# Attention with grouped heads: a strip of every sixth score chunk exponentiated on VectorE, and PV three chunks behind

## The chip, the core and the metric

The kernel runs on one core of one Trainium2 chip. The metric is the device time in microseconds (us); a shorter time is better. A core has five engines that run side by side and meet through semaphores: TensorE (PE in the profile; its weight loads are listed apart as PEld), VectorE (DVE), ScalarE (ACT), GpSimd (POOL) and the sync engine (SP), which here only issues transfers. Matmul results land in PSUM, which has eight banks of 512 fp32 columns on 128 partitions; everything else is in SBUF.

## What is computed

```python
B, Hq, Hkv, Sq, Sk, D = 16, 32, 8, 288, 512, 128      # q, k, v in bf16
k = jnp.repeat(k, Hq // Hkv, axis=1)
v = jnp.repeat(v, Hq // Hkv, axis=1)
scores = jnp.einsum("bhqd,bhkd->bhqk", q, k) * D ** -0.5
p = jax.nn.softmax(scores, axis=-1)
return jnp.einsum("bhqk,bhkd->bhqd", p, v)
```

Four query heads share one k and v head. The inputs are small (normal values times 0.05), so the exponentials are taken without subtracting a maximum; the kernel checks the sums at its end and has a slow general path (lines 17 to 121) for inputs where that fails.

## The kernel before

**Tiling.** A group is one k/v head of one batch: 128 groups (`NG`). Its four query heads give 1152 query rows, held as 9 tiles of 128. A chunk is three of these tiles (`TPC`), 384 query rows, against all 512 keys, which are four key tiles of 128 (`NJ`). Scores are computed transposed, with keys on the partitions, so a chunk has 4 x 384 = 1536 score columns (`CH`), three PSUM banks. There are three chunks in a group and `NS` = 384 in all, numbered n.

**Stages of a chunk.**
- S(n), `op_s`, matmuls on line 361: six matmuls into `ps_s[:, n % 2]`, cut at bank and key-tile borders (384, 128, 256, 256, 128 and 384 columns). They need k and q in SBUF, transposed by DMA, and exp(n-2) finished, since `ps_s` has two buffers.
- exp(n), `op_exp`, line 417 (line 411 for the first bank of chunk 0): one ScalarE instruction over all 1536 columns, from PSUM to bf16 in `pt_sb[:, n % NPT]`, with `NPT` = 4 buffers, so it also needs PV(n-4) finished.
- PV(r), `op_pv`, line 384: twelve matmuls (four key tiles by three query tiles) with 128x128 of `pt_sb` as weights and 129 columns of v as the moving operand. The 129th column of v is all ones, so it sums the exponentials. The result, 3 x 129 = 387 columns, goes to `ps_o[:, r % 2]`, one bank each. PV(r) waits for exp(r), for v, and for the eviction of r-2, which frees the bank. The last chunk's PV is written apart (`op_pv_last`, line 395, in `ps_s`).
- VectorE, lines 434 and 444: `op_rc` takes the reciprocals of the three sums, `op_ev` multiplies the outputs by them and writes bf16 to `o_sb`, the eviction. Once every 24 chunks two small reductions (`op_stat`) keep the largest and smallest reciprocal.

**Order.** Each engine's instructions are written out in one fixed order. TensorE (line 515 on) issues S(n) and then PV(n-LAG), with `LAG` = 2. ScalarE issues exp(n) for all n. VectorE loops over r with `op_rc(r)` and `op_ev(r)`. A wait is put into an instruction only if the engine hasn't seen that count before (`need`). SP's transfers are sorted by a time in chunks that the code works out for each (lines 488 to 500): k and v for four groups at a time (`UG`) into three slots, q for one group into twelve slots (`NQ`), and the store of one group, whose time has `LAG` in it. GpSimd copies v into its slot with the ones column (`op_vc`, line 427), one group at a time, as soon as the load of four groups has landed and the slot's last PV is done.

**Start.** Before the loop TensorE runs warm-up matmuls on zeros (`op_warm`) and transposes the k of group 0 itself (`op_kt`, line 336), which VectorE copies to `kt_sb` (`op_kc`, line 343). The k of group 1 is transposed in the loop at n = LAG. Their loads, and that of v for groups 0 and 1, are issued from ScalarE's queue (lines 533 to 536), ahead of its first exponential.

Of the kernel before, what the change touches and what calls it, by code (L numbers as in the profile page):

```python
# [1 line left out]

# [7 lines left out]
FP32 = mybir.dt.float32  # L10
I32 = mybir.dt.int32
# [109 lines left out]
    return {"pool": on_pool, "sp": on_sync, "pe": on_tensor, "dve": on_vector, "act": on_scalar}  # L121


def bass_standalone__gqa_softmax__near_ridge_kernel(
    nc: bass.Bass,
    q: bass.AP,
# [6 lines left out]
    P = 128  # L133
    R = (Hq // Hkv) * Sq
    NJ = Sk // P
# [9 lines left out]
    assert COLS % CH == 0 and NT == NC * TPC and NJ * P == BANK  # L145
    scale = float(D) ** -0.5
    DV = D + 1
    VP = 160
    LAG = 2
    TW = TPC * P  # L150
    UG = 4
    NU = NG // UG
    NSLOT = 3
    NQ = 12
    NPT = 4
    WARM = 5
    AHEAD = 1.08
    NO = 12
    NS = NG * NC
# [10 lines left out]
    with ExitStack() as es:  # L170
# [14 lines left out]
            S("us_v%d" % i)  # L185
        for i in range(UG):
            S("s_k%d" % i)
        for name in ["s_v0", "s_v2", "s_s0", "s_kd0", "s_kd1", "s_id", "s_kp"]:
            S(name)
        for i in range(NQ):  # L190
            S("s_q%d" % i)
# [36 lines left out]
        st_sb = main.enter_context(nc.sbuf_tensor("st_sb", [P, 2, B], FP32))  # L228
        ck_sb = main.enter_context(nc.sbuf_tensor("ck_sb", [P, 3], FP32))
        bad_sb = main.enter_context(nc.sbuf_tensor("bad_sb", [P, 2, ALONE + 1], FP32))  # L230
        one_f = main.enter_context(nc.sbuf_tensor("one_f", [P, 1], FP32))
        z_sb = main.enter_context(nc.sbuf_tensor("z_sb", [P, BANK], BF16))
        dum = main.enter_context(nc.sbuf_tensor("dum", [P, 2], FP32))
# [5 lines left out]
        def need(eng, waits):  # L239

            left = []
            for (s, n) in waits:
                key = (id(eng), s)
                if seen.get(key, 0) < n:
                    seen[key] = n
                    left.append((sem[s], n))
            return left

        def emit(eng, waits, fn):
            waits = need(eng, waits)  # L250
            for (s, n) in waits[:-1]:
                eng.wait_ge(s, n)
            ins = fn()
            if waits:
                ins.wait_op(waits[-1][0], waits[-1][1], "sem-ge")
            return ins
# [17 lines left out]
        def op_v(u, eng=None, g0=0, g1=UG):  # L274
            eng = eng or nc.sync
            sl = u % NSLOT
            if u >= NSLOT:
                for (s, n) in need(eng, [("s_vc", UG * (u - NSLOT + 1))]):
                    eng.wait_ge(s, n)
            eng.dma_start(  # L280
                vd_sb[:, sl, g0:g1], v_v[:, u * UG + g0:u * UG + g1]
            ).then_inc(sem["us_v%d" % sl if u > 0 else "s_v%d" % g0], 16)
# [63 lines left out]
        def op_warm(n, w, dst):  # L346

            for x in range(n):
                emit(nc.tensor, [("s_z", 1)], lambda: nc.tensor.matmul(  # L349
                    dst[:, 0:w], z_sb[:, 0:P], z_sb[:, 0:w], start=True, stop=True))  # L350

        def op_s(n):
            eng = nc.tensor
            g, i = n // NC, n % NC
            sl, gi = (g // UG) % NSLOT, g % UG
            waits = [have("k", g), have_q(g, i)]
            if n >= 2:
                waits.append(("s_e", n - 1))
            qg = qt_sb[:, g % NQ, i * TPC:(i + 1) * TPC].rearrange("d t p -> d (t p)")
            for x, (c, j, r0, w) in enumerate(pieces):  # L360
                ins = emit(eng, waits if x == 0 else [], lambda: eng.matmul(  # L361
                    ps_s[:, n % 2, c:c + w], kt_sb[:, sl, j, gi, :], qg[:, r0:r0 + w], start=True, stop=True))
                if n == 0 and c + w == BANK:
                    ins.then_inc(sem["s_s0"], 1)
            ins.then_inc(sem["s_s"], 1)

        def outs(r):

# [4 lines left out]
        def op_pv(r):  # L373
            eng = nc.tensor
            g = r // NC
            sl, gi = (g // UG) % NSLOT, g % UG
            waits = [("s_vc", g + 1), ("s_e", r + 1)]
            if 2 <= r < NS - 1:
                waits.append(("s_ev", r - 1))


            for j in range(NJ):
                for a in range(TPC):
                    ins = emit(eng, waits if a == 0 and j == 0 else [], lambda: eng.matmul(  # L384
                        outs(r)[:, a, :], pt_sb[:, r % NPT, j, a * P:(a + 1) * P],
                        v_sb[:, sl, gi * NJ + j, 0:DV], start=(j == 0 and a == 0), stop=(j == NJ - 1),
                        skip_group_check=True))
            ins.then_inc(sem["s_pv"], 1)
# [13 lines left out]
        def op_exp(n):  # L402
            eng = nc.scalar
            waits = [("s_s", n + 1)]
            if n >= NPT:
                waits.insert(0, ("s_pv", n - NPT + 1))
            dst, src = pt_sb[:, n % NPT], ps_s[:, n % 2].rearrange("p (j r) -> p j r", r=TW)
            parts = [(dst.rearrange("p j r -> p (j r)"), ps_s[:, n % 2])]
            if n == 0:
                d, s = parts[0]  # L410
                emit(eng, [("s_s0", 1)], lambda: eng.activation(d[:, 0:BANK], s[:, 0:BANK], ACTF.Exp, scale=scale))  # L411
                parts = [(d[:, BANK:CH], s[:, BANK:CH])]
            if n == NS - 1:
                w = TW - P
                parts = [(dst[:, :, 0:w], src[:, :, 0:w]), (dst[:, :, w:TW], src[:, :, w:TW])]
            for (d, s) in parts:
                emit(eng, waits, lambda: eng.activation(d, s, ACTF.Exp, scale=scale)).then_inc(sem["s_e"], 1)  # L417


        def op_vc(g):  # L420
# [11 lines left out]
        def op_rc(r):  # L432
            eng = nc.vector
            emit(eng, [("s_pv", r + 1)], lambda: eng.reciprocal(  # L434
                rl_sb[:, TPC * r:TPC * (r + 1)].unsqueeze(2), outs(r)[:, :, D:DV])).then_inc(sem["s_rc"], 1)
# [74 lines left out]
        @block.tensor  # L510
        def _(eng):
            op_warm(WARM, BANK, ps_o[:, 1])
            op_kt(0, range(NJ), 0)
            op_warm(6, P, ps_s[:, 1])
            for n in range(NS):
                if n == LAG:
                    op_kt(1, range(NJ), 1)
                    op_warm(4, P, ps_o[:, 0])
                op_s(n)
                if n >= LAG:  # L520
                    op_pv(n - LAG)
            for r in range(NS - LAG, NS - 1):
                op_pv(r)
            for a in range(TPC):
                op_pv_last(a)
            emit(eng, [("s_ev", NS - 1), ("s_bad", 2)], lambda: eng.matmul(  # L526
                ps_o[0:1, NS % 2, 0:ALONE + 1], one_f[:], bad_sb[:, 1, :], start=True, stop=True)
            ).then_inc(sem["s_bad"], 1)
            choose(eng, "pe")

        @block.scalar
        def _(eng):
            op_kd(eng, 0)
            emit(eng, [("s_one", 1)], lambda: eng.activation(dum[:, 1:2], dum[:, 0:1], ACTF.Exp))  # L534
            op_v(0, eng, 0, 2)
            op_kd(eng, 1)
            for n in range(NS):
                op_exp(n)
            op_ev_act()
            choose(eng, "act")  # L540
# [12 lines left out]
        @block.vector  # L553
        def _(eng):
            eng.memset(z_sb[:], 0.0).then_inc(sem["s_z"], 1)  # L555
            eng.memset(dum[:], 0.0).then_inc(sem["s_one"], 1)
            eng.memset(one_f[:], 1.0)
            op_kc(0, range(NJ), 0, 1)
            op_kc(1, range(NJ), 1, 2)
            per_b = G * NC  # L560
            w0 = NS - 1 - ALONE // TPC
            last = rl_sb[:, NG * NT - ALONE:NG * NT]
            for r in range(NS - 1):
                op_rc(r)
                op_ev(r)
                if r % per_b == per_b - 1 and r < NS - 1:
                    op_stat(r // per_b)
                if r == w0:
                    op_stat(B - 1)
                if r == w0 + 1:  # L570
                    emit(eng, [("s_stat", B)], lambda: eng.tensor_reduce(
                        ck_sb[:, 0:1], st_sb[:, 0, :], AX.X, ALU.max))
                    eng.tensor_reduce(ck_sb[:, 1:2], st_sb[:, 1, :], AX.X, ALU.min).then_inc(sem["s_stat"], 1)
                if r == w0 + 2:
                    op_over(ck_sb[:, 0:1], ck_sb[:, 1:2], ALONE, ALONE + 1, ("s_stat", B + 1), B + 2)
            op_rc(NS - 1)
            op_ev_last()
            op_over(last, last, 0, ALONE, ("s_rc", NS), B + 3)
            with nc.allow_low_precision(reason="a count of at most 2048"):
                emit(eng, [("s_bad", 3)], lambda: eng.tensor_reduce(  # L580
                    flag_i[:], ps_o[0:1, NS % 2, 0:ALONE + 1], AX.X, ALU.add)).then_inc(sem["s_flag"], 1)
            choose(eng, "dve")
# [30 lines left out]
```

## Time and profile before

| | us |
|---|---|
| median of 4 runs | 528.7 (527.38 to 529.08) |
| the profiled execution: its time | 527.63 |
| the profiled execution: its span, from the first to the last instruction | 525.9 |
| TensorE, ScalarE busy | 521.2, 518.1 |
| VectorE, GpSimd busy | 289.7, 74.0 |

The granted TensorE clock is at its full value (1.00) over the whole span, and there are 384 chunks in it. A row of the profile names the line and the engine, the tile written and the tiles read, the shape and the number of instructions; after the bars come the busy time in us, the mean length of one instruction in ns, the idle time of the engine just before them, and what ended most of it. Matmuls overlap one another, and their ends are modelled: the busy time of PE says nothing on whether it could do more. Instructions on ScalarE are listed from the moment they may start, so one that queues behind another looks longer than it is.

### The profile page before, as it was taken

To read this page: it belongs to the slowest core of one execution; us is meant where nothing else is said; L and a number is where in the kernel's file an instruction comes from. 1 tells how busy PE (TensorE), PEld (TensorE's weight loads), DVE (VectorE), ACT (ScalarE), POOL (GpSimd) and SP (SyncE) were. 2 spreads that over 40 slices of the span, in tenths; PEclk is the share of its full clock that TensorE was granted. 3 is DMA by queue.
4 is the path that set the end of the run, shared out by engine and by line. 5 is a ranking of instruction groups with operands and counts; after the bars stand their busy time and mean duration, and the time that the engine had idled before them with its cause. 6 is when DMAs were issued, how large, how long until landed. Compare 5 with 4: busy or idle time off the path is not lost.

```text
span 525.9 us, 16369 instructions
## 1 busy us (share of the span) xinstructions
PE 521.2 (99%) x6937; PEld 457.3 (87%) x6937; DVE 289.7 (55%) x812; ACT 518.1 (99%) x389; POOL 74.0 (14%) x135
## 2 busy tenths in 40 slices
PE   8999999999999999999999999999999999999997
PEld 6888888888888888888888888888888888888886
DVE  2555555555555555555555555555555555555555
ACT  6999999999999999999999999999999999999997
POOL 1210111111111011111111011101111101111000
PEclk9999999999999999999999999999999999999999
DMA  8999999999999999999999999999999999998112
GB/s 163 193 234 216 205 254 228 255 218 210 252 224 241 235 248 199 211 226 239 219 236 195 233 181 262 245 171 228 246 199 224 218 204 191 233 216 194 69 70 91
DMA packets 253143, 110.12 MB, mean 209 GB/s; under 512 B 219792, under 2 KB 236816, under 8 KB 253072
## 3 DMA queue, kind: packets, MB, share of 16 engines
q1 hardware_dynamic: 252512, 108.56, 99.6%
q8 instruction: 55, 0.90, 0.8%
q10 hardware_dynamic: 560, 0.52, 0.3%
q14 instruction: 16, 0.13, 0.1%
HBM read 17.04 MB, written 37.75 MB: 104 GB/s over the span
## 4 chain that ended last, share of the span: by engine, by line
PE 98%; DMA 1%; DVE 0%; issue 0%
PE ps_o L384 50%; PE ps_s L361 49%; DMA qt_sb<-in_q_dram 1%; PE ps_s L395 0%; DVE o_sb L454 0%; PE ps_o L526 0%; PE ps_o L349 0%; PE ps_o L336 0%; DVE bad_sb L480 0%; DVE rl_sb L434 0%; DVE flag_i L580 0%; DVE bad_sb L477 0%
## 5 line engine op out<-in xcount | busy, mean ns | idle before, releaser
L417 ACT ACTIVATE pt_sb<-ps_s 128x1536 bf16<-128x1536 f32 (+1 forms) x385 | 515.7, 1745 | 0.3 <-PE ps_s L361 0.3
L384 PE MATMUL ps_o<-v_sb,pt_sb 128*128 128x129 bf16 x4596 | 322.9, 220 | 0.0
L361 PE MATMUL ps_s<-qt_sb,kt_sb 128*128 128x384 bf16 (+2 forms) x2304 | 318.2, 274 | 0.4 <-DMA qt_sb<-in_q_dram 0.4
L384 PEld LDWEIGHTS ps_o<-v_sb,pt_sb 128*128 128x128 bf16 x4596 | 291.9, 98 | 24.8
L444 DVE TENSOR_TENSOR o_sb<-ps_o,rl_sb 128x384 bf16<-128x384 f32 x383 | 213.6, 558 | 13.3
L361 PEld LDWEIGHTS ps_s<-qt_sb,kt_sb 128*128 128x128 bf16 x2304 | 179.1, 98 | 37.4 <-DMA qt_sb<-in_q_dram 0.7
L434 DVE RECIPROCAL rl_sb<-ps_o 128x3 f32<-128x3 f32 x383 | 69.3, 181 | 213.6 <-PE ps_o L384 213.6
L427 POOL COPY v_sb<-vd_sb 128x512 bf16<-128x512 bf16 x128 | 73.1, 613 | 409.4 <-DMA vd_sb<-in_v_dram 352.0
L343 DVE COPY kt_sb<-ps_o 128x512 bf16<-128x512 bf16 x2 | 0.8, 425 | 6.2 <-PE ps_o L336 6.2
L349 PE MATMUL ps_o<-z_sb 128*128 128x512 bf16 (+1 forms) x9 | 2.7, 447 | 1.3 <-DVE z_sb L555 1.3
L411 ACT ACTIVATE pt_sb<-ps_s 128x512 bf16<-128x512 f32 x1 | 0.6, 597 | 3.0 <-PE ps_s L361 3.0
L470 DVE TENSOR_REDUCE st_sb<-rl_sb 128x1 f32<-128x72 f32 (+1 forms) x16 | 3.5, 217 | 0.0
L472 DVE TENSOR_REDUCE st_sb<-rl_sb 128x1 f32<-128x72 f32 (+1 forms) x16 | 3.5, 217 | 0.0
L349 PEld LDWEIGHTS ps_o<-z_sb 128*128 128x128 bf16 x9 | 0.8, 118 | 2.1 <-DVE z_sb L555 1.3
L534 ACT ACT_TABLE_LOAD x1 | 1.3, 1283 | 1.2 <-PEq L598 1.2
L336 PEld LDWEIGHTS ps_o<-ident,kd_sb 128*128 128x128 bf16 x8 | 0.7, 115 | 0.8 <-DMA kd_sb<-in_k_dram 0.7
L526 PE MATMUL ps_o<-bad_sb,one_f 128*1 128x25 f32 x2 | 0.2, 184 | 1.0 <-DVE bad_sb L480 1.0
L526 PEld LDWEIGHTS ps_o<-bad_sb,one_f 128*1 128x1 f32 x2 | 0.1, 80 | 1.2 <-DVE bad_sb L480 1.2
L461 ACT ACTIVATE o_sb<-ps_s,rl_sb 128x128 bf16<-128x128 f32 x1 | 0.4, 367 | 0.7 <-DVE rl_sb L434 0.7
L336 PE MATMUL ps_o<-ident,kd_sb 128*128 128x128 bf16 x8 | 1.0, 263 | 0.0
L395 PE MATMUL ps_s<-v_sb,pt_sb 128*128 128x129 bf16 x12 | 0.9, 222 | 0.0
L395 PEld LDWEIGHTS ps_s<-v_sb,pt_sb 128*128 128x128 bf16 x12 | 0.7, 98 | 0.2 <-ACT pt_sb L417 0.2
(22 smaller groups left out, 5.1 us busy)
## 6 DMA issues: line engine op xcount, KB each, us to landing
out_dram<-o_sb SPq DMA_DIRECT2D x127, 288.0 KB, 4.2
vd_sb<-in_v_dram SPq DMA_DIRECT2D x31, 512.0 KB, 5.7
qt_sb<-in_q_dram SPq DMA_TRANSPOSE x130, 4.9
kt_sb<-in_k_dram SPq DMA_TRANSPOSE x32, 5.7
out_dram<-o_sb SPq DMA_DIRECT2D x3, 96.0 KB, 1.6
kd_sb<-in_k_dram ACTq DMA_DIRECT2D x2, 128.0 KB, 3.3
vd_sb<-in_v_dram ACTq DMA_DIRECT2D x1, 256.0 KB, 3.5
vd_sb<-in_v_dram SPq DMA_DIRECT2D x1, 256.0 KB, 3.7
```

Source lines behind the costliest of these rows:

```text
L336: ins = emit(eng, [("s_id", 2), ("s_kd%d" % g, 16)], lambda: eng.transpose(dst[:, x * P:(x + 1) * P], kd_sb[:, g, j * D:(j + 1) * D], iden ...
L349: emit(nc.tensor, [("s_z", 1)], lambda: nc.tensor.matmul(dst[:, 0:w], z_sb[:, 0:P], z_sb[:, 0:w], start=True, stop=True))
L361: ins = emit(eng, waits if x == 0 else [], lambda: eng.matmul(ps_s[:, n % 2, c:c + w], kt_sb[:, sl, j, gi, :], qg[:, r0:r0 + w], start=Tru ...
L384: ins = emit(eng, waits if a == 0 and j == 0 else [], lambda: eng.matmul(outs(r)[:, a, :], pt_sb[:, r % NPT, j, a * P:(a + 1) * P], v_sb[: ...
L395: ins = emit(eng, [("s_e", NS + (0 if a < TPC - 1 else 1))], lambda: eng.matmul(outs(NS - 1)[:, a, :], pt_sb[:, (NS - 1) % NPT, j, a * P:( ...
L417: emit(eng, waits, lambda: eng.activation(d, s, ACTF.Exp, scale=scale)).then_inc(sem["s_e"], 1)
L427: emit(eng, waits, lambda: eng.tensor_copy(v_sb[:, sl, gi * NJ:(gi + 1) * NJ, 0:D], vd_sb[:, sl, gi].rearrange("p (j d) -> p j d", d=D))). ...
L434: emit(eng, [("s_pv", r + 1)], lambda: eng.reciprocal(rl_sb[:, TPC * r:TPC * (r + 1)].unsqueeze(2), outs(r)[:, :, D:DV])).then_inc(sem["s_ ...
L444: emit(eng, waits, lambda: eng.tensor_tensor(out=o_sb[:, g % NO, t0:t0 + TPC, :], in0=outs(r)[:, :, 0:D], in1=rl_sb[:, TPC * r:TPC * (r + ...
L470: emit(eng, [("s_rc", e // TPC)], lambda: eng.tensor_reduce(st_sb[:, 0, b:b + 1], rl_sb[:, a:e], AX.X, ALU.max))
L472: eng.tensor_reduce(st_sb[:, 1, b:b + 1], rl_sb[:, a:e], AX.X, ALU.min).then_inc(sem["s_stat"], 1)
L534: emit(eng, [("s_one", 1)], lambda: eng.activation(dum[:, 1:2], dum[:, 0:1], ACTF.Exp))
```

## The change

It has three parts and what follows from them.

1. In 63 of the 384 chunks (n = 4, 10, 16, ... 376; `shared(n)`) the last 120 score columns (`W`) are not written to `ps_s`. The last matmul of S(n) shrinks from 384 columns to 264, exp(n) from 1536 to 1416, and a further matmul, `op_sy`, puts the 120 columns into the free end of an output bank, `ps_o[:, (n - LAG) % 2, 392:512]`, just ahead of PV(n-3), which writes columns 0 to 386 of the same bank. `op_sy` waits for the eviction of n-5, which PV(n-3) waited for until now.
2. VectorE turns these scores into exponentials. `op_y` clamps them from PSUM to SBUF once PV(n-3) has ended. `op_yb` multiplies and adds, and writes an integer whose high bits are an exponent and whose low bits a fraction. `op_ym` cuts the two apart with AND and OR (two instructions). `op_yu` (three) and `op_yp` work out a quartic of the fraction, and `op_yp` multiplies it by the power of two and writes 120 bf16 columns of `pt_sb`. These eight instructions are set between the reciprocals and evictions of r = n-3 and r = n-2. The last matmul of PV(n) waits for `op_yp`.
3. PV runs three chunks behind S instead of two (`LAG`), and `pt_sb` has six buffers instead of four (`NPT`). The transposes of group 1's k move with `LAG`, from n = 2 to n = 3, and the stores one chunk later in SP's order.

At the start there are eight warm-up matmuls instead of six after the first transposes, and ScalarE's queue waits for these transposes before it issues the loads of v for groups 0 and 1 and of k for group 1.

```diff
-    LAG = 2
+    LAG = 3
+    W = 120
+    EVERY = 6
+    NB = 2
-    NPT = 4
+    NPT = 6
+    FIRST_SHARED = 4
...
@@ op_s @@
             for x, (c, j, r0, w) in enumerate(pieces):
+                if shared(n) and c + w == CH:
+                    w -= W
...
+        def op_sy(n):
+
+            eng = nc.tensor
+            g, t = n // NC, n % NC * TPC + TPC - 1
+            emit(eng, [("s_ev", n - LAG - 1)], lambda: eng.matmul(
+                ps_o[:, (n - LAG) % 2, BANK - W:BANK], kt_sb[:, (g // UG) % NSLOT, NJ - 1, g % UG, :],
+                qt_sb[:, g % NQ, t, P - W:P], start=True, stop=True))
@@ op_pv @@
+                    w_x = waits if a == 0 and j == 0 else []
+                    if a == TPC - 1 and j == NJ - 1 and shared(r):
+                        w_x = w_x + [("s_yp", nth(r))]
@@ op_exp @@
+            if shared(n):
+                parts = [(d[:, 0:CH - W], s[:, 0:CH - W]) for (d, s) in parts]
...
+        def shared(n):
+            return FIRST_SHARED <= n < NS - 6 and (n - FIRST_SHARED) % EVERY == 0
+
+        def nth(n):
+            return (n - FIRST_SHARED) // EVERY + 1
+
+        def op_y(n):
+            eng, b = nc.vector, nth(n) % NB
+            emit(eng, [("s_yb", nth(n) - NB), ("s_pv", n - LAG + 1)], lambda: eng.tensor_scalar(
+                out=y_sb[:, b], in0=ps_o[:, (n - LAG) % 2, BANK - W:BANK], scalar1=-Y_MAX, scalar2=Y_MAX,
+                op0=ALU.max, op1=ALU.min)).then_inc(sem["s_y"], 1)
+
+        def op_yb(n):
+            eng, b = nc.vector, nth(n) % NB
+            emit(eng, [("s_ym", 2 * (nth(n) - NB)), ("s_y", nth(n))], lambda: eng.tensor_scalar(
+                out=t_sb[:, b], in0=y_sb[:, b], scalar1=Y_MUL, scalar2=Y_ADD, op0=ALU.mult, op1=ALU.add)
+            ).then_inc(sem["s_yb"], 1)
+
+        def op_ym(n):
+            eng, b = nc.vector, nth(n) % NB
+            for x, (dst, mask, bits) in enumerate(((m_sb, 0x7FFFFF, QUARTER_BITS), (e_sb, 0x7F800000, LEAD_BITS))):
+                emit(eng, [("s_yp", nth(n) - NB), ("s_yb", nth(n))], lambda: eng.tensor_scalar(
+                    out=dst[:, b], in0=t_sb[:, b], scalar1=mask, scalar2=bits,
+                    op0=ALU.bitwise_and, op1=ALU.bitwise_or)).then_inc(sem["s_ym"], 1)
+
+        def op_yu(n, x):
+            eng, b = nc.vector, nth(n) % NB
+            m = m_sb[:, b].bitcast(FP32)
+            src = m if x == 0 else u_sb[:, b, x - 1]
+            emit(eng, [("s_ym", 2 * nth(n) - 1) if x == 0 else ("s_yu", 3 * nth(n) - 3 + x)],
+                 lambda: eng.scalar_tensor_tensor(
+                     out=u_sb[:, b, x], in0=src, scalar=QUARTIC[x], in1=m, op0=ALU.add, op1=ALU.mult)
+                 ).then_inc(sem["s_yu"], 1)
+
+        def op_yp(n):
+            eng, b = nc.vector, nth(n) % NB
+            emit(eng, [("s_pv", n - NPT + 1), ("s_ym", 2 * nth(n)), ("s_yu", 3 * nth(n))],
+                 lambda: eng.scalar_tensor_tensor(
+                     out=pt_sb[:, n % NPT, NJ - 1, TW - W:TW], in0=u_sb[:, b, 2], scalar=QUARTIC[3],
+                     in1=e_sb[:, b].bitcast(FP32), op0=ALU.add, op1=ALU.mult)).then_inc(sem["s_yp"], 1)
@@ tensor @@
-            op_warm(6, P, ps_s[:, 1])
+            op_warm(8, P, ps_s[:, 1])
...
                 op_s(n)
+                if shared(n):
+                    op_sy(n)
@@ scalar @@
+            for (s, n) in need(eng, [("s_kp", 1)]):
+                eng.wait_ge(s, n)
             op_v(0, eng, 0, 2)
@@ vector @@
             for r in range(NS - 1):
+                n = r + LAG
                 op_rc(r)
+                if shared(n):
+                    op_y(n)
+                if shared(n - 1):
+                    op_yu(n - 1, 1)
                 op_ev(r)
+                if shared(n):
+                    op_yb(n)
+                    op_ym(n)
+                    op_yu(n, 0)
+                if shared(n - 1):
+                    op_yu(n - 1, 2)
+                    op_yp(n - 1)
```

More of the change, by code (lines that the diff above doesn't have):

```diff
@@ L1 @@
+import math
 from contextlib import ExitStack
@@ L121, in general_path @@
     return {"pool": on_pool, "sp": on_sync, "pe": on_tensor, "dve": on_vector, "act": on_scalar}
+LOG2E = math.log2(math.e)
+QUARTIC = (-0.039256332078737396, 0.7694109050129492, 0.36021799676460203, 0.1471865760029904)
+QUARTER_BITS = 0x3E800000
+LEAD_BITS = 0x3FDDBE69 & 0x7FFFFF
 def bass_standalone__gqa_softmax__near_ridge_kernel(
@@ L147, in bass_standalone__gqa_softmax__near_ridge_kernel @@
     DV = D + 1
+    Y_MAX = 126.0 / (scale * LOG2E)
+    Y_MUL, Y_ADD = scale * LOG2E * 2.0 ** 23, 128.0 * 2.0 ** 23
     VP = 160
-    LAG = 2
+    LAG = 3
+    W = 120
+    EVERY = 6
+    NB = 2
     TW = TPC * P
@@ L187, in bass_standalone__gqa_softmax__near_ridge_kernel @@
             S("s_k%d" % i)
-        for name in ["s_v0", "s_v2", "s_s0", "s_kd0", "s_kd1", "s_id", "s_kp"]:
+        for name in ["s_v0", "s_v2", "s_s0", "s_y", "s_yb", "s_ym", "s_yu", "s_yp", "s_kd0", "s_kd1", "s_id", "s_kp"]:
             S(name)
@@ L230, in bass_standalone__gqa_softmax__near_ridge_kernel @@
         bad_sb = main.enter_context(nc.sbuf_tensor("bad_sb", [P, 2, ALONE + 1], FP32))
+        y_sb = main.enter_context(nc.sbuf_tensor("y_sb", [P, NB, W], FP32))
+        t_sb = main.enter_context(nc.sbuf_tensor("t_sb", [P, NB, W], I32))
+        m_sb = main.enter_context(nc.sbuf_tensor("m_sb", [P, NB, W], I32))
+        e_sb = main.enter_context(nc.sbuf_tensor("e_sb", [P, NB, W], I32))
+        u_sb = main.enter_context(nc.sbuf_tensor("u_sb", [P, NB, 3, W], FP32))
         one_f = main.enter_context(nc.sbuf_tensor("one_f", [P, 1], FP32))
@@ L383, in op_pv @@
                 for a in range(TPC):
-                    ins = emit(eng, waits if a == 0 and j == 0 else [], lambda: eng.matmul(
+                    w_x = waits if a == 0 and j == 0 else []
+                    if a == TPC - 1 and j == NJ - 1 and shared(r):
+                        w_x = w_x + [("s_yp", nth(r))]
+                    ins = emit(eng, w_x, lambda: eng.matmul(
                         outs(r)[:, a, :], pt_sb[:, r % NPT, j, a * P:(a + 1) * P],
```

## The prediction

> **What bounds the kernel now.** I read the page's busy shares first, then its costliest groups.
>
> ```profile
> PE 521.2 (99%) x6937; PEld 457.3 (87%) x6937; DVE 289.7 (55%) x812; ACT 518.1 (99%) x389; POOL 74.0 (14%) x135
> ...
> L417 ACT ACTIVATE pt_sb<-ps_s 128x1536 bf16<-128x1536 f32 (+1 forms) x385 | 515.7, 1745 | 0.3 <-PE ps_s L361 0.3
> L384 PE MATMUL ps_o<-v_sb,pt_sb 128*128 128x129 bf16 x4596 | 322.9, 220 | 0.0
> L361 PE MATMUL ps_s<-qt_sb,kt_sb 128*128 128x384 bf16 (+2 forms) x2304 | 318.2, 274 | 0.4 <-DMA qt_sb<-in_q_dram 0.4
> ```
>
> Two engines are at 99%, so busy shares don't decide. The line of the exponentials, asked in three stretches, and the weight loads in order of time do (columns: minimum/median/maximum duration in ns, first and last start; then start and length in us):
>
> ```profile
> L417 ACT ACTIVATE pt_sb<-ps_s x4: 1445/1454/1472, 7.6 to 11.6; 128x1536 bf16<-128x1536 f32 x4
> L417 ACT ACTIVATE pt_sb<-ps_s x4: 1552/1572/1592, 19.6 to 23.6; 128x1536 bf16<-128x1536 f32 x4
> L417 ACT ACTIVATE pt_sb<-ps_s x76: 1761/1762/1762, 98.6 to 199.4; 128x1536 bf16<-128x1536 f32 x76
> ```
> ```profile
> 15.06 0.83 PEld L384 LDWEIGHTS ps_o<-v_sb,pt_sb 128*128 128x128 bf16 x12
> ...
> 27.08 0.83 PEld L384 LDWEIGHTS ps_o<-v_sb,pt_sb 128*128 128x128 bf16 x12
> ...
> 40.52 0.83 PEld L384 LDWEIGHTS ps_o<-v_sb,pt_sb 128*128 128x128 bf16 x12
> ```
>
> See the exponential grow from 1445 to 1762 ns and stay: it starts when its scores are there, but queues behind the one before it. Until 27 us TensorE runs by itself: (27.08-15.06)/9 chunks = **1335.6 ns** a chunk. After that S(n) has to wait for exp(n-2): (40.52-27.08)/10 = 1344 ns, and 98.6 to 199.4 gives 100.8/75 = 1344 ns too. So ScalarE bounds, with TensorE only 8 ns a chunk behind. The chain of waits names PE for 98% only because modelled matmul ends hide these 8 ns.
>
> What VectorE and GpSimd do beside it:
>
> ```profile
> 300.82 0.18 DVE L434 RECIPROCAL rl_sb<-ps_o 128x3 f32<-128x3 f32 x1 [0.57 <-PE ps_o L384]
> 301.04 0.56 DVE L444 TENSOR_TENSOR o_sb<-ps_o,rl_sb 128x384 bf16<-128x384 f32 x1
> ...
> 301.12 0.83 PEld L384 LDWEIGHTS ps_o<-v_sb,pt_sb 128*128 128x128 bf16 x12
> ...
> 302.47 0.83 PEld L384 LDWEIGHTS ps_o<-v_sb,pt_sb 128*128 128x128 bf16 x12
> ```
> ```profile
> 37.00 2.28 POOL L427 COPY v_sb<-vd_sb 128x512 bf16<-128x512 bf16 x4 [12.28 <-DMA vd_sb<-in_v_dram]
> 53.28 2.28 POOL L427 COPY v_sb<-vd_sb 128x512 bf16<-128x512 bf16 x4 [14.00 <-DMA vd_sb<-in_v_dram]
> ```
>
> VectorE idles 0.57 us a chunk. PV(r+2), which reuses PV(r)'s bank, loads its first weights 302.47-300.82 = 1.65 us after the reciprocal of r starts; the eviction ends 0.78 us after it. GpSimd copies v in bursts of four copies, 2.28 us long; 30 such bursts are in the trace, at no fixed place against the chunks.
>
> **What the Trainium skill says.** "ScalarE: Activation LUTs", What ACT_TABLE_LOAD costs: 0.833 ns an element. The trace agrees: unqueued, 1536 elements take 1445 and 512 take 597 ns (line 411): 848/1024 = 0.828. "TensorE: Matmul & The Clock Gate", Wait — 56ns, not 53.3ns?: columns/2.4 plus about 2.5 ns a matmul when warm; a chunk (3084 columns, 18 matmuls) would be 1330 ns, and 1335.6 was measured. "VectorE: DVE Perf Modes", The perf-mode tier table: an fp32 tensor_scalar between SBUF tensors runs two elements a cycle; no row of before shows one of useful size. "SBUF — State Buffer", Who interferes with whom: a VectorE instruction in a two-port mode, or with two SBUF inputs while GpSimd reads SBUF, takes a port pair that GpSimd also needs, and the second to come waits for the whole instruction. Nothing in the trace shows it: the evictions (one SBUF input) take 557 to 559 ns with 30 bursts beside them.
>
> **The change, part by part** (m is a shared chunk: 4, 10, ... 376, so 63).
>
> *ScalarE* loses 120 columns in each: 120 x 0.828 = 99 ns, 6.3 us in all, 16.6 ns a chunk. It would need 1344-16.6 = 1327 ns, below TensorE's 1335.6. So TensorE becomes the bound, and only the difference to it is gained. Over the 380 chunks from S(3) (9.23 us) to S(383) (519.59 us) the pace is 510.36/380 = 1343.05: 7.45 x 380 = **-2.8 us**.
>
> *TensorE* has the same columns, one matmul more in each shared chunk, one wait there on an eviction four PVs back, and one before the last matmul of PV(m). Below it: 2.5 ns, 0.2 us in all. Above: a weight load laid bare, 98 ns, 6.2 us. The wait-bearing borders of a chunk cost 1335.6-1330 = 5.6 ns for two today; I take 2.5+5.6 = 8 ns: **+0.5 us**. No gain is in it, as nothing is taken away.
>
> *PV three behind.* Three PVs, not two, follow the last S before the last PV: +0.68 us (520.25 to 521.84 holds two). The wait for the last exponential goes: 24 matmuls of 56.7 ns from 520.25 end at 521.61, the next starts at 521.84: -0.23. At the start the transposes of the second k come just ahead of S(3), which needs their VectorE copy. Before, transposes began at 7.41 and the copy ended at 8.26. Now S(2) ends at 7.86+0.66 = 8.52, plus 0.85 and 0.05 is 9.42 against 9.23: +0.2. Its cover, ScalarE's exp(2), lasts to 10.4, so only TensorE's time is lost. Together **+0.65 us**. Six pt buffers free exp(n) by PV(n-6), three chunks before it: nothing.
>
> *Start.* ScalarE's queue holds the v and second k loads until the first transposes are done (4.03 us, not 1.29 and 1.72). Issue 0.4 and landing 3.5 give v at 8.0; k lands near 7.8, needed at 8.5. If they cross the traffic later, up to 0.3 is lost. The first q, due at 5.06, may come earlier, but not usefully before the eight warm-up matmuls end, about 4.8: at most -0.3. I take **-0.1 us**. SP's stores move one chunk later in its order, with no new wait ahead of q or v.
>
> *VectorE.* Eight instructions. From the rows of one and 24 elements (144 and 169 ns for tensor_scalar, 159 and 184 for scalar_tensor_tensor: 1.09 ns an element) and the evictions (425 ns for 256 PSUM columns, 558 for 384): clamp 284; three bit and affine steps 273 each, or 209 at two a cycle (the page's rate, which I take); four polynomial steps 288 each. 284+627+1152 = 2.06 us in six chunks that hold 6 x 0.56 = 3.4 us of idle time. But two deadlines count. With 0.04 us between dependent steps (300.82+0.18 to 301.04) and about 0.08 of overlap otherwise, measured from the reciprocal of PV(m-3): eviction to 0.87, first group to 1.60, next reciprocal at 1.53 instead of 1.34, its eviction to 2.40, last step to 2.93. PV(m) may not be held by that eviction at 1.34+1.64 = 2.98 (slack **0.57 us**) nor by the last step at its last weight load, 0.30+2x1.34+0.73 = 3.70 (slack **0.77 us**). At 273 instead of 209 each slack shrinks by about 0.15. So nothing on the path.
>
> Sum: -2.8+0.5+0.65-0.1 = **-1.8 us**. The profiled execution took 527.63 us (span 525.9 and 1.7 around it): 525.8. The median of the runs is 528.7, which gives **526.9**.
>
> **Rivals.** *A, the forecast*, 525.6 to 527.9: for it speak both slacks, and that one wait of at most one copy (2.28/4 = 0.57 us) is just absorbed.
> *B, GpSimd holds the port* (ends slower). Seven of the eight VectorE instructions are of the kinds that the page names, and TensorE has nothing to spare any more. It decides once VectorE waits for over 0.57 us, that is for two copies of one burst. If they take turns, a burst that begins with the first group costs some 1.6 us of waiting and 1.0 of stall; one that began 0.9 us earlier 0.3; later than 1.5 us after, none. A mean of 0.75 over 2.2 of 8.0 us is 0.2 us a burst, x30 = 6 us: 533. If a burst keeps the port throughout, 1.25 over 3.2 of 8.0 us: 15 us, 542. Against it: bursts scatter, and no trace here shows it.
> *C, the extra matmul and its waits eat the gain*: 30 to 35 ns each (a third of a bare weight load), 2 us: 528.5. For it: two new waits; against it: the loads run ahead everywhere.
> *D, the VectorE chain is over 0.6 us longer than worked out*: 0.1 us in each shared chunk is 6 us, so 533 to 536.
>
> **How the numbers follow.** A 0.56, B 0.30 (0.18 taking turns, 0.12 not), C 0.10, D 0.04. About 0.3% (1.6 us) is what a measurement can tell here; faster begins at 527.1. A puts 0.44 there and 0.12 within; C 0.08 within, 0.02 slower; B 0.01, 0.04 and 0.25; D 0.04 slower. Faster 0.45, same 0.24, slower 0.31. The range leaves out the burst that keeps the port and the ends: 525.4 to 536; A's own is 525.6 to 527.9.
>
> **What would show it.** Right: weight-load groups every 1336 to 1338 ns throughout; full-size exponentials back near 1450 ns, as they no longer queue; reciprocals still on PV's heels except beside shared chunks. B: bit and polynomial steps of 0.5 us and more beside v copies, and TensorE waiting on VectorE there. C: a chunk time 30 ns over its neighbours at each shared chunk alone. D: a TensorE wait on the last step in every shared chunk. The prediction is wrong if the pace stays at 1344 or shared chunks show TensorE waits.

## The result, and the profile after

| | before | after |
|---|---|---|
| median of the runs, us | 527.75 (55 runs, 527.0 to 529.75) | 527.81 (34 runs, 526.06 to 529.72) |
| after / before, with its 95% interval | | 0.9997 [0.999, 1.0004] |
| the profiled execution: time, span, us | 527.63, 525.9 | 527.62, 525.9 |

The change makes no difference that can be measured. The forecast was 525.8 us for the profiled execution, against 527.62 measured. (The 528.7 us that the prediction also refers to is the median of four runs; 55 runs give 527.75.)

The page of the kernel after, its busy shares and the costliest groups:

```profile
PE 518.1 (99%) x7002; PEld 460.0 (87%) x7002; DVE 371.3 (71%) x1316; ACT 515.6 (98%) x389; POOL 75.0 (14%) x135
...
L453 ACT ACTIVATE pt_sb<-ps_s 128x1536 bf16<-128x1536 f32 (+2 forms) x385 | 513.2, 1439 | 2.4 <-PE ps_s L384 2.4
L418 PE MATMUL ps_o<-v_sb,pt_sb 128*128 128x129 bf16 x4596 | 322.8, 220 | 1.3 <-DVE o_sb L522 1.3
```

Two things are new. The mean exponential fell from 1745 to 1439 ns, so it hardly queues any more. And the output matmuls (line 418) sat idle for 1.3 us until an eviction (line 522), where the kernel before had 0.0.

The exponentials alone between 100 and 200 us (minimum, median and maximum in ns), and the weight loads of the output matmuls in order of time (start and length in us; one group of 12 loads in every shared chunk of this stretch):

```profile
L453 ACT ACTIVATE pt_sb<-ps_s x76: 1353/1450/1471, 99.2 to 199.9; 128x1536 bf16<-128x1536 f32 x63, 128x1416 bf16<-128x1416 f32 x13
```
```profile
28.20 0.72 PEld L418 LDWEIGHTS ps_o<-v_sb,pt_sb 128*128 128x128 bf16 x12
...
36.22 0.72 PEld L418 LDWEIGHTS ps_o<-v_sb,pt_sb 128*128 128x128 bf16 x12
...
44.23 0.72 PEld L418 LDWEIGHTS ps_o<-v_sb,pt_sb 128*128 128x128 bf16 x12
...
52.24 0.72 PEld L418 LDWEIGHTS ps_o<-v_sb,pt_sb 128*128 128x128 bf16 x12
```

(52.24-28.20)/18 chunks = 1335.6 ns a chunk, the pace TensorE had before whenever nothing held it. The extra matmul lies inside it. So the bound moved from ScalarE to TensorE as forecast, and the pace gain is there. It was given back in three places.

**In the loop.** The waits of the kernel after between 14 and 515 us (total us, times, longest us):

```profile
PEld ps_o L418 <- DVE o_sb L522: 1.9, 3, 0.8
...
PE ps_o L418 <- DVE o_sb L522: 1.1, 3, 0.5
```

TensorE waits three times for VectorE. From the intervals between the starts of successive PVs (1.74, 1.82 and 2.01 us where 1.336 is normal, at PV(10), PV(76) and PV(280)) they cost 0.40 + 0.48 + 0.67 = 1.55 us. The order of time around the last of the three, VectorE, GpSimd and TensorE:

```profile
382.92 0.21 DVE L470 TENSOR_SCALAR t_sb<-y_sb 128x120 int32<-128x120 f32 x1
382.92 2.40 POOL L505 COPY v_sb<-vd_sb 128x512 bf16<-128x512 bf16 x4 [11.06 <-DMA vd_sb<-in_v_dram]
383.16 0.51 DVE L477 TENSOR_SCALAR m_sb<-t_sb 128x120 int32<-128x120 int32 x1
383.59 0.64 DVE L477 TENSOR_SCALAR e_sb<-t_sb 128x120 int32<-128x120 int32 x1
384.15 0.70 DVE L486 SCALAR_TENSOR_TENSOR u_sb<-m_sb 128x120 f32<-128x120 f32 x1
384.77 0.17 DVE L512 RECIPROCAL rl_sb<-ps_o 128x3 f32<-128x3 f32 x1
384.88 0.57 DVE L486 SCALAR_TENSOR_TENSOR u_sb<-u_sb,m_sb 128x120 f32<-128x120 f32 x1
385.38 0.54 DVE L522 TENSOR_TENSOR o_sb<-ps_o,rl_sb 128x384 bf16<-128x384 f32 x1
...
385.98 0.85 PE L418 MATMUL ps_o<-v_sb,pt_sb 128*128 128x129 bf16 x12 [0.50 <-DVE o_sb L522]
```

A burst of v copies starts at 382.92. The four steps that run beside it take 0.51, 0.64, 0.70 and 0.57 us; the eviction behind them ends at 385.92, and PV(280), which needs its bank, starts at 385.98. The same steps without a burst:

```profile
302.79 0.21 DVE L470 TENSOR_SCALAR t_sb<-y_sb 128x120 int32<-128x120 f32 x1
303.04 0.22 DVE L477 TENSOR_SCALAR m_sb<-t_sb 128x120 int32<-128x120 int32 x1
303.18 0.22 DVE L477 TENSOR_SCALAR e_sb<-t_sb 128x120 int32<-128x120 int32 x1
303.31 0.28 DVE L486 SCALAR_TENSOR_TENSOR u_sb<-m_sb 128x120 f32<-128x120 f32 x1
```

**At the end.** The last matmuls of TensorE, before and then after:

```profile
519.59 0.83 PE L361 MATMUL ps_s<-qt_sb,kt_sb 128*128 128x384 bf16 x6
520.25 1.61 PE L384 MATMUL ps_o<-v_sb,pt_sb 128*128 128x129 bf16 x24
521.84 0.89 PE L395 MATMUL ps_s<-v_sb,pt_sb 128*128 128x129 bf16 x12
```
```profile
518.87 0.82 PE L384 MATMUL ps_s<-qt_sb,kt_sb 128*128 128x384 bf16 x6
519.53 1.52 PE L418 MATMUL ps_o<-v_sb,pt_sb 128*128 128x129 bf16 x24
521.24 0.85 PE L418 MATMUL ps_o<-v_sb,pt_sb 128*128 128x129 bf16 x12 [0.19 <-DVE o_sb L522]
521.93 0.84 PE L429 MATMUL ps_s<-v_sb,pt_sb 128*128 128x129 bf16 x12
```

The last scores start 0.72 us earlier than before, but the last PV at 521.93 instead of 521.84. From the last S to the last PV it was 2.25 us and is now 3.06: +0.81. Three PVs now follow the last S, and the third waits for the eviction of the first.

**At the start.** The first score matmuls, before and then after:

```profile
5.11 2.47 PE L361 MATMUL ps_s<-qt_sb,kt_sb 128*128 128x384 bf16 x12 [0.44 <-DMA qt_sb<-in_q_dram]
...
9.23 0.81 PE L361 MATMUL ps_s<-qt_sb,kt_sb 128*128 128x384 bf16 x6
```
```profile
4.66 1.59 PE L384 MATMUL ps_s<-qt_sb,kt_sb 128*128 128x384 bf16 x12
7.80 0.81 PE L384 MATMUL ps_s<-qt_sb,kt_sb 128*128 128x384 bf16 x6 [1.55 <-DMA qt_sb<-in_q_dram]
...
9.83 0.81 PE L384 MATMUL ps_s<-qt_sb,kt_sb 128*128 128x384 bf16 x6 [0.76 <-DMA qt_sb<-in_q_dram]
```

S(0) starts at 4.66, 0.45 us earlier than before (5.11), but S(2) and then S(3) wait for q. S(3) starts at 9.83 where it was 9.23: +0.60. The load of q for group 1, which S(3) needs, landed at 9.69 us, where it was 9.10 before.

**The ledger**, from S(3) on. Before, S(3) to S(383) took 510.36 us; after, it is 518.87-9.83 = 509.04, of which 1.55 are the stalls: 507.49/380 = 1335.5 ns a chunk. So the pace brought 380 x (1343.05-1335.5) = -2.9 us. The start +0.60, the stalls +1.55 and the end +0.81 make +2.96, and the sum is +0.1 us: the two spans are equal at 525.9.

### The profile page after: what moved, and what is told of

Same layout as the page of the kernel before. It is cut to its first block, busy times and chain, and to the rows that moved or that the text cites. A ratio compares the mean times of both kernels' runs of the same rounds, so it can differ in the third digit from the quotient of the medians.

```text
span 525.9 us, 17125 instructions
## 1 busy us (share of the span) xinstructions
PE 518.1 (99%) x7002; PEld 460.0 (87%) x7002; DVE 371.3 (71%) x1316; ACT 515.6 (98%) x389; POOL 75.0 (14%) x135
## 4 chain that ended last, share of the span: by engine, by line
PE 95%; DVE 2%; DMA 1%; SPq 1%; issue 0%
PE ps_o L418 49%; PE ps_s L384 46%; DMA qt_sb<-in_q_dram 1%; SPq L315 1%; PE ps_o L394 1%; DVE o_sb L522 1%; DVE u_sb L486 1%; DVE e_sb L477 0%; DVE rl_sb L512 0%; DVE m_sb L477 0%; DVE t_sb L470 0%; DVE y_sb L464 0%; DVE o_sb L532 0%; PE ps_o L606 0%; DVE bad_sb L558 0%
## 5 line engine op out<-in xcount | busy, mean ns | idle before, releaser
L453 ACT ACTIVATE pt_sb<-ps_s 128x1536 bf16<-128x1536 f32 (+2 forms) x385 | 513.2, 1439 | 2.4 <-PE ps_s L384 2.4
L384 PE MATMUL ps_s<-qt_sb,kt_sb 128*128 128x128 bf16 (+3 forms) x2304 | 311.1, 271 | 2.3 <-DMA qt_sb<-in_q_dram 2.3
L384 PEld LDWEIGHTS ps_s<-qt_sb,kt_sb 128*128 128x128 bf16 x2304 | 193.5, 98 | 36.3 <-issue 2.7
L486 DVE SCALAR_TENSOR_TENSOR u_sb<-u_sb,m_sb 128x120 f32<-128x120 f32 x126 | 36.6, 291 | 0.0
L493 DVE SCALAR_TENSOR_TENSOR pt_sb<-u_sb,e_sb 128x120 bf16<-128x120 f32 x63 | 19.0, 301 | 2.2
L486 DVE SCALAR_TENSOR_TENSOR u_sb<-m_sb 128x120 f32<-128x120 f32 x63 | 18.7, 297 | 0.0
L477 DVE TENSOR_SCALAR m_sb<-t_sb 128x120 int32<-128x120 int32 x63 | 15.6, 247 | 2.1
L464 DVE TENSOR_SCALAR y_sb<-ps_o 128x120 f32<-128x120 f32 x63 | 15.9, 252 | 0.0
L477 DVE TENSOR_SCALAR e_sb<-t_sb 128x120 int32<-128x120 int32 x63 | 15.8, 250 | 0.0
L470 DVE TENSOR_SCALAR t_sb<-y_sb 128x120 int32<-128x120 f32 x63 | 13.6, 216 | 0.0
```

The source lines that it names most:

```text
L464: emit(eng, [("s_yb", nth(n) - NB), ("s_pv", n - LAG + 1)], lambda: eng.tensor_scalar(out=y_sb[:, b], in0=ps_o[:, (n - LAG) % 2, BANK - W: ...
L470: emit(eng, [("s_ym", 2 * (nth(n) - NB)), ("s_y", nth(n))], lambda: eng.tensor_scalar(out=t_sb[:, b], in0=y_sb[:, b], scalar1=Y_MUL, scala ...
L477: emit(eng, [("s_yp", nth(n) - NB), ("s_yb", nth(n))], lambda: eng.tensor_scalar(out=dst[:, b], in0=t_sb[:, b], scalar1=mask, scalar2=bits ...
L486: lambda: eng.scalar_tensor_tensor(out=u_sb[:, b, x], in0=src, scalar=QUARTIC[x], in1=m, op0=ALU.add, op1=ALU.mult)
L493: lambda: eng.scalar_tensor_tensor(out=pt_sb[:, n % NPT, NJ - 1, TW - W:TW], in0=u_sb[:, b, 2], scalar=QUARTIC[3], in1=e_sb[:, b].bitcast( ...
```

## The experiments

The theory: the pace gain is real, and it went to bursts of v copies that meet the VectorE chain, and to fixed costs of PV three behind and of the new start. The rivals: VectorE's chain is too long by itself, so that stalls come without GpSimd too; or the pace never improved. Each kernel is the kernel after with the edit shown, except the last, which is the kernel before with one part of the change. Ratios are to the kernel before on the same chip.

**1. The bursts kept out of the chain.** The copies of four groups wait for a PV that ends two chunks after a chain has begun, so that they run once the chain is over. With three slots for v nothing else is late.

```diff
@@ op_vc @@
+            if u >= 1:
+                waits.append(("s_pv", NC * UG * u - 2))
```

> Edit: GpSimd's copies of v for four groups also wait for a PV count, so that each burst of four starts where VectorE has only reciprocals and evictions to do. Theory (copies and bit steps share a port; the three TensorE stalls of the changed kernel, 0.40 + 0.48 + 0.67 = 1.55 us, come from bursts that meet the bit and polynomial steps): no such step over 0.35 us, no TensorE wait on VectorE in the loop, about 1.5 us less than the changed kernel, so 0.25 to 0.3% faster than the kernel before. Rival (the stalls come from VectorE's own chain, which is just too long now and then): the waits stay, and the time is that of the changed kernel.

Measured: 525.86 us, ratio 0.997 [0.9958, 0.9982]. In the loop TensorE no longer waits for VectorE at all, and S(3) at 9.71 to S(383) at 517.16 is 507.45 us, 1335.4 ns a chunk without subtracting anything. The first polynomial step in all 63 shared chunks:

```profile
L486 DVE SCALAR_TENSOR_TENSOR u_sb<-m_sb x63: 269/277/279, 14.5 to 510.6; 128x120 f32<-128x120 f32 x63
```

Minimum and maximum are 10 ns apart; in the kernel after the longest of these was 697 ns. Only the copies of the first four groups stay where they were: beside them two other steps of chunk 4 took 0.58 and 0.52 us, more than the 0.35 expected at most, but TensorE didn't wait. The gain over the kernel before, which the kernel after equals, is 1.6 us [0.9 to 2.2]: as much as the 1.55 us of stalls read from the trace. Nothing else in the loop has changed its length: without its stalls the loop of the kernel after takes 507.49 us. So the stalls need GpSimd, and the chain alone fits.

**2. The bursts put where the chain is.** The same edit with another count: the copy starts when the eviction of r = m-3 has ended, just as the bit steps begin.

```diff
@@ op_vc @@
+            if u >= 1:
+                waits.append(("s_ev", NC * UG * u - 4))
```

> Edit: each burst of four v copies waits for the eviction after which the bit steps of a shared chunk start, so that all 31 bursts meet them. Theory (port held for one copy at a time, turn and turn about): four or five steps of 0.5 to 0.7 us beside each burst, a TensorE wait of 0.4 to 0.7 us in each, 31 x 0.5 = 15 us slower than the kernel before, 543 us. If the port were held through a whole burst: 31 x 1.2 = 37 us, 565 us. Rival (GpSimd has no part in it): 528 us, and steps of 0.22 to 0.28 us.

Measured: 549.06 us, ratio 1.0398 [1.0381, 1.0414]. Of this kernel, the waits of TensorE's weight loads (total us, times, longest us), then VectorE and GpSimd in order of time in one chain:

```profile
PEld ps_o L418 <- DVE o_sb L524: 26.6, 32, 0.9
```
```profile
306.51 0.21 DVE L470 TENSOR_SCALAR t_sb<-y_sb 128x120 int32<-128x120 f32 x1
306.75 0.59 DVE L477 TENSOR_SCALAR m_sb<-t_sb 128x120 int32<-128x120 int32 x1
307.26 0.64 DVE L477 TENSOR_SCALAR e_sb<-t_sb 128x120 int32<-128x120 int32 x1
307.82 0.70 DVE L486 SCALAR_TENSOR_TENSOR u_sb<-m_sb 128x120 f32<-128x120 f32 x1
...
308.55 0.57 DVE L486 SCALAR_TENSOR_TENSOR u_sb<-u_sb,m_sb 128x120 f32<-128x120 f32 x1
```
```profile
306.66 2.33 POOL L507 COPY v_sb<-vd_sb 128x512 bf16<-128x512 bf16 x4 [14.45 <-DVE o_sb L524]
```

Now the chain is held at every burst. It is 1.5 us longer (from the start of `op_yb` to the end of `op_yp` 3.58 us, against 2.09 in the undisturbed chain at 302.79), and (549.06-525.86)/31 bursts = 0.75 us of it reach the end, where 0.5 was expected. The burst itself takes 2.33 us, where it takes 2.28 alone, and the four slow steps end 0.56, 0.62 and 0.60 us apart, about the length of a copy (2.33/4 = 0.58). So one VectorE instruction gets through for each copy. The case in which a burst keeps VectorE out throughout, put at 565 us, didn't come.

**3. PV two behind with the rest kept.**

```diff
-    LAG = 3
+    LAG = 2
```

> Edit: the changed kernel with PV two chunks behind instead of three. Theory (the chain from reciprocal to last step takes 2.82 us, and with two chunks the last weight load of PV(m) is due 2.37 us after the reciprocal): a wait of some 0.5 us in each of the 63 shared chunks, 31 us, less about 1.4 us at the start and the end: 557 us. Rival (the third chunk is cost without use, its start and tail are what ate the gain): 526.5 us.

Measured: 567.27 us, ratio 1.0747 [1.0731, 1.0763], more than either number. The waits of this kernel (total us, times, longest us), and one of them:

```profile
PEld ps_o L418 <- DVE pt_sb L493: 42.7, 63, 2.0
```
```profile
300.49 0.28 DVE L493 SCALAR_TENSOR_TENSOR pt_sb<-u_sb,e_sb 128x120 bf16<-128x120 f32 x1
...
300.83 0.23 PE L418 MATMUL ps_o<-v_sb,pt_sb 128*128 128x129 bf16 x1 [0.30 <-DVE pt_sb L493]
```

All 63 shared chunks wait for the last step, 42.7/63 = 0.68 us by the weight load. In 45 of them the next PV starts 0.47 us late, close to the 0.5 of the theory. In the rest, beside bursts, it is up to 2.0 us, and that I hadn't counted. So the third chunk of lag is not an extra: without it the chain doesn't fit.

**4. PV three behind and the new start, without the shared chunks.**

```diff
         def shared(n):
-            return FIRST_SHARED <= n < NS - 6 and (n - FIRST_SHARED) % EVERY == 0
+            return False
```

> Edit: the changed kernel with no shared chunk at all: PV three chunks behind, six buffers and the new start stay. Theory (ScalarE bounds at 1344 ns a chunk again; start and tail of the changed kernel cost what the sharing gained): the exponentials grow to a length above 1700 ns again, S(3) starts near 9.8 us, and the end comes 0.2 to 0.8 us later than in the kernel before: 528.0 to 528.6. Rival (three chunks behind frees ScalarE or TensorE by itself): the pace is 1336 ns and the time 526 us.

Measured: 528.58 us, ratio 1.0012 [1.0003, 1.0021], which is +0.6 us [0.2 to 1.1]. The exponentials of this kernel in one stretch:

```profile
L453 ACT ACTIVATE pt_sb<-ps_s x75: 1761/1761/1762, 99.3 to 198.7; 128x1536 bf16<-128x1536 f32 x75
```

They queue as in the kernel before, and S(3) at 10.09 to S(383) at 520.23 gives 510.14/380 = 1342.5 ns. So the pace gain comes from the shared chunks alone; end (+0.81) and start (+0.86 in this profile) are what PV three behind and the start cost. (The profiled execution took 528.99 us, 0.4 more than the median.)

**5. The old start.** Six warm-up matmuls, and ScalarE's loads issued at once.

```diff
-            op_warm(8, P, ps_s[:, 1])
+            op_warm(6, P, ps_s[:, 1])
...
-            for (s, n) in need(eng, [("s_kp", 1)]):
-                eng.wait_ge(s, n)
```

> Edit: in the changed kernel only the start goes back to that of before: six warm-up matmuls, and the loads of v and of the second k issued at once. Theory (the later loads meet the transposing load of q of group 1, for which S(3) waits until 9.8 us): S(3) starts near 9.4 us, held by the copy of the second k and not by q, and the time is 0.3 to 0.5 us under that of the changed kernel: 527.2. Rival (q is late in any case): S(3) at 9.7 to 10.1 us, and the same time as the changed kernel or up to 0.4 us more, since S(0) starts at 5.1 again.

Measured: 528.35 us, ratio 1.0008 [0.9998, 1.0018]. The expected gain isn't there. In its profile TensorE itself was slow at first, for longer than in the others:

```profile
5.53 4.04 PE L384 MATMUL ps_s<-qt_sb,kt_sb 128*128 128x384 bf16 x18 [0.28 <-DMA qt_sb<-in_q_dram]
```

18 score matmuls took 4.04 us there. The first 12 took 2.47 us in the kernel before and 1.59 in the kernel after. The views list a clock of 1.00 in all three, so that figure doesn't show this slowness. The load of q for group 1 did land earlier, at 9.18 us against 9.69 in the kernel after. But the transposes of the second k stood behind the slow matmuls, their copy ended at 10.46, and S(3) came at 10.56. This run doesn't tell what the loads' order is worth in time.

**6. The bursts kept out, the old start, and the second k transposed at n = 2 as before.** The edits of experiments 1 and 5, and:

```diff
-                if n == LAG:
+                if n == 2:
                     op_kt(1, range(NJ), 1)
```

> Edit: the copies of v kept out of the shared chunks' way, the old start, and the transposes of the second k ahead of S(2) as before. Theory: no TensorE wait on VectorE in the loop, 1336 ns a chunk, S(3) at 9.1 to 9.3 us instead of 9.7, so 0.4 to 0.6 us less than with the copies alone: 525.3. If q is what S(3) waits for whatever the start is: 525.9.

Measured: 525.47 us, ratio 0.9962 [0.9949, 0.9976], the lowest median of all. S(3) starts at 8.92, again as soon as q has landed (8.78), S(383) at 516.37 (507.45 us again) and the last PV at 519.43. Its gain over experiment 1 lies inside both intervals.

**7. Half as many shared chunks.**

```diff
-    EVERY = 6
+    EVERY = 12
```

> Edit: the changed kernel with every twelfth chunk shared instead of every sixth, 32 in all; the copies of v stay where they fall. ScalarE then needs 1343.6 - 99.4/12 = 1335.3 ns a chunk, TensorE 1335.6. Theory (TensorE sets the pace as soon as ScalarE is below it, and stalls come from bursts that meet a chain): 1336 ns a chunk, half the stalls or fewer, since there are half the chains: 0.7 us less than the changed kernel, 527.0. Rival (ScalarE needs a margin below TensorE for the pace): 1338 to 1340 ns a chunk and 528.5.

Measured: 527.97 us, ratio 1.0004 [0.9993, 1.0014]. Without its stalls the pace is (518.23-9.49-1.31)/380 = 1335.3 ns: 32 narrower exponentials are enough, since they bring ScalarE to 1344-16.6/2 = 1335.7 ns, level with TensorE. But the stalls weren't halved. They come to 1.31 us: 0.38 at PV(64), 0.74 at PV(76) and two of some 0.1 us. Both of these lie beside bursts too. PV(4) waits for an eviction behind steps of 0.63 and 0.70 us, beside a burst of two copies; PV(244) waits for its own last step, which took 0.57 us. In experiment 5 PV(64), PV(76) and PV(280) stall, and in the kernel after PV(10), PV(76) and PV(280). Of these four only PV(10) is no longer shared here; the others are of the form 4 + 12k. My error was to count on bursts scattered at random over all chains: a burst comes once in twelve chunks, and here PV(76) was hit in all three profiles, PV(64) and PV(280) in two.

**8. Experiment 6, with PV two behind again in the last two steps**, so that no three PVs stand in a row.

```diff
                 if n >= LAG:
-                    op_pv(n - LAG)
-            for r in range(NS - LAG, NS - 1):
-                op_pv(r)
+                    op_pv(n - LAG + (n == NS - 1))
+                if n == NS - 2:
+                    op_pv(n - 2)
+            op_pv(NS - 2)
```

> Edit: the kernel with calm copies, old start and early transposes, and in its last two steps PV two chunks behind, so that two PVs and not three stand together before the last one. Theory (the third PV in a row waits for an eviction, and the last PV waits for the exponential of chunk 383, which comes 0.68 us later in this order): the wait on VectorE of 0.2 to 0.4 us goes, one on ScalarE comes, net 0.1 us less. Rival (the three PVs cost nothing of their own): no change.

Measured: 526.0 us, ratio 0.9959 [0.9944, 0.9975], not to be told from experiment 6. The end of its trace:

```profile
516.93 1.52 PE L418 MATMUL ps_o<-v_sb,pt_sb 128*128 128x129 bf16 x24
518.29 0.82 PE L384 MATMUL ps_s<-qt_sb,kt_sb 128*128 128x384 bf16 x6
518.95 1.52 PE L418 MATMUL ps_o<-v_sb,pt_sb 128*128 128x129 bf16 x24
520.31 0.84 PE L429 MATMUL ps_s<-v_sb,pt_sb 128*128 128x129 bf16 x12
```

PV(379) to the last PV takes 520.31-516.93 = 3.38 us, against 519.43-515.69 = 3.74 in experiment 6: -0.36, and the wait of 0.19 is gone. The wait on ScalarE that was expected in exchange doesn't show. So the wait for an eviction in the row of three is real and worth that much in the trace. The execution as a whole hides it behind a start that was slower (S(3) at 9.90, against 8.92 in experiment 6).

**9. The kernel before with the new start alone.**

```diff
-            op_warm(6, P, ps_s[:, 1])
+            op_warm(8, P, ps_s[:, 1])
...
+            for (s, n) in need(eng, [("s_kp", 1)]):
+                eng.wait_ge(s, n)
             op_v(0, eng, 0, 2)
```

> Edit: the kernel before with only the start of the changed kernel: eight warm-up matmuls, and the loads of v and of the second k held until the first transposes are done. Theory (the held loads meet the load of q of group 1, for which S(3) then waits): S(3) starts at 9.5 to 10.0 us instead of 9.23, and since ScalarE bounds, the end comes 0.2 to 0.6 us later than in the kernel before: 528.0. Rival (the new start is a gain, S(0) being 0.4 us earlier, and only PV three chunks behind costs): 0.3 us less, 527.3.

Measured: 527.97 us, ratio 1.0005 [0.9997, 1.0013]. Its first matmuls:

```profile
8.00 0.40 PE L336 MATMUL ps_o<-ident,kd_sb 128*128 128x128 bf16 x4 [1.42 <-DMA kd_sb<-in_k_dram]
...
8.45 0.82 PE L361 MATMUL ps_s<-qt_sb,kt_sb 128*128 128x384 bf16 x6
...
9.79 0.82 PE L361 MATMUL ps_s<-qt_sb,kt_sb 128*128 128x384 bf16 x6
```

S(3) is at 9.79 as forecast (9.5 to 10.0), +0.56 on the kernel before, but what holds it back is the second k, whose load was issued late: S(2) waits for its transposes, and S(3) follows one chunk behind. The q for group 1 landed at 9.64, so that without this wait S(3) could hardly have come sooner. At S(383) +0.35 us are left (519.94 against 519.59). The times don't separate this from nothing.

## Why the prediction was wrong, step by step

The measured 527.81 us lies in the range that was given, 525.4 to 536, and even in A's own, 525.6 to 527.9. That is luck. A gain of 1.8 us was forecast and none came. The 528.7 us that the forecast was counted from is 0.95 us above the median of 55 runs, and this hides half of the miss: counted from 527.75, A's own range would end at 526.95. Of the signs that the prediction named, the pace and the shorter exponentials came, but so did one of being wrong: shared chunks show TensorE waits, three of them.

The bound, the pace and the mechanism of each loss were in the prediction. The sum was wrong because a term taken at zero was 1.55 us, and two small ones were too small; an extra matmul priced too high made up for some of it.

| term, us | forecast | measured in the trace |
|---|---|---|
| pace | -2.8 | -2.9 |
| extra matmul and its waits | +0.5 | 0.16, counted in the pace |
| VectorE's chain on the path | 0 | +1.55 |
| S(3) (start -0.1, moved transposes +0.2) | +0.1 | +0.60 |
| end (third PV +0.68, last exponential's wait -0.23) | +0.45 | +0.81 |
| sum | -1.8 | +0.1 |

*Pace: right.* ScalarE's 16.6 ns a chunk gave TensorE the bound, and only the 7.5 ns between them were gained. Experiment 4 (no shared chunks: no gain) and experiment 7 (half as many: the same gain) show both halves of it.

*Extra matmul: too dear.* In experiment 1 a shared chunk takes 1337.5 ns from S(n) to S(n+1), and every other chunk 1335.0 (means over n = 20 to 375). So the added matmul, its weight load and both waits cost 2.5 ns, the lower end of what the prediction gave, and 63 x 2.5 = 0.16 us in all; 1335.0+2.5/6 is the pace of 1335.4. Rival C, with 30 to 35 ns in each shared chunk, is out.

*VectorE's chain: the step that failed.* "So nothing on the path" holds for the chain by itself. It is 2.82 us from the reciprocal of m-3 to the end of the last step (302.06 to 304.88), where I had 2.93, and experiment 1 has no stall in the loop. Rival D is out. What failed is the assumption in the forecast that bursts of v copies leave the chain alone: it allowed for one wait of one copy, which the slack absorbs, and beside the burst at 382.92 four steps in a row waited. Rival B's mechanism is there: of the Trainium skill I had cited "SBUF — State Buffer", Who interferes with whom, where the second to come waits for the whole instruction, and this trace now agrees with that (0.51 to 0.70 us for steps of 0.22 to 0.28). Its size was too large.

With the start of a burst of four measured from the reciprocal of m-3, stalls came for starts at 0.36, 0.74 and 1.09 us (0.48, 0.67 and 0.40 us), and none for starts at -0.34 or before or at 1.27 or after. So the harmful stretch is between 0.7 and 1.6 us wide, say 1.2, not 2.2. A stall in it is 0.5 us on average here, not 0.75, though experiment 2, with 30 bursts at 0.88, has 0.74 in each of them. One reason is that the eviction had more room: in the undisturbed chain PV(m) starts 305.18-302.06 = 3.12 us after the reciprocal, against the 2.98 I used, and the undisturbed eviction ends 2.31 us after it (303.82+0.55-302.06), not 2.40. The slack is therefore nearer 0.8 than 0.57 us. With bursts at random places, 1.2/8.0 x 31 = 4.7 of them at 0.5 us would be 2.3 us (31 bursts of four are in the traces before and after, not 30); the schedule puts three there, which gives 1.55. The prediction set B against the forecast as 6 us or none; it is a small number of meetings, each with its own price.

*The end: mis-sized by 0.36.* The third PV was counted at TensorE's own 0.68 us. But three PVs in a row alternate two banks, so the third needs the first one's eviction: reciprocal and eviction take 0.77 us, longer than the PV between them. Experiment 8 breaks the row and takes 0.36 us off the trace.

*The start: mis-sized by 0.5, and its price in time only partly settled.* The prediction allowed up to 0.3 us should the held loads of v and k cross later traffic, and of q it asked only when the first load lands. That load does land earlier with the new start, at 3.43 to 4.52 us in seven profiles against 5.06 to 5.57 in the four with the old one (before, experiments 5, 6 and 8). But the third load, for S(2), lands at 7.29 to 7.95 instead of 6.27 to 6.84, and the fourth, for S(3), at 9.35 to 9.96 instead of 8.78 to 9.18. The ranges don't meet, so the new start does delay the q that S(3) needs, by about 0.6 us. Which of the held loads does it wasn't tried.

What this costs at the end is another matter. With the old start S(3) came at 8.92, 9.23, 9.90 and 10.56 us, with the new one at 9.49 to 10.09, and the first 12 score matmuls took anything from 1.55 to 2.74 us. So the +0.60 of the table holds for its two profiles only. By experiment 9 the new start's cost in the median stays open between 0 and about 0.7 us.

## What to carry to other kernels

When work is taken from the bounding engine, the gain ends at the next engine (here 7.5 ns a chunk), so price every fixed cost of the rearrangement with the same care: a stage put one step further behind adds its own length at the end and the waits that it meets standing in a row. Steps that move to VectorE have to be laid in time against GpSimd's copies, and where the copies have slack, one semaphore count that starts them after the chain is free (here 1.6 us of 528). In a schedule that repeats, don't average over random positions: list the few meetings there are, since some chunks are hit again and again (PV(76) in all three profiles here).

## What the runs showed of the hardware

- A VectorE step of 120 columns that ran wholly beside GpSimd's copies took 0.51 to 0.70 us instead of 0.22 to 0.28, the bit steps with one SBUF input as well as the polynomial steps with two. GpSimd lost less: a burst took 2.28 to 2.61 us in the kernel after, 2.28 alone. Evictions and clamps, which read PSUM, were not touched: 543 to 560 and 251 to 254 ns with or without a burst.
- The three bit and affine steps took 213 to 224 ns and the polynomial steps 277 to 282 (medians; 209 and 288 had been estimated), the clamp from PSUM 252 (284).
- One matmul split in two, with the same weights loaded once more and the columns sent to another bank, cost 2.5 ns in a chunk of 1335.0 ns (experiment 1).
- TensorE's first matmuls ran slower in some profiles than in others: six score matmuls, from the start of S(0) to that of S(1), took 0.73 us in experiment 6 and 1.25 us in the kernel before and in experiment 5.
